# Sums of w2's quarters in the last three experts: ScalarE copies and adding DMAs in place of GpSimd additions

## The chip, the core and the metric

The kernel runs on one core of a Trainium2 chip. A core has TensorE (PE, matrix products), VectorE (DVE), ScalarE (ACT), GpSimd (POOL) and SyncE (SP), which work side by side and wait for each other through semaphores, and 16 DMA engines that move data. DMAs are issued by SP, ACT or POOL. The metric is the device time of one execution in microseconds.

## The reference

The program is an attention block without a softmax followed by a layer of eight experts.

```python
kv = np.einsum('bhsd,bhse->bhde', k, v)
out = np.einsum('bhsd,bhde->bhse', q, kv)
x = out / sqrt(mean(out * out) + 1e-6) * g_norm      # then reshaped to 4608 rows of 512
logits = x @ w_gate                                  # 4608 x 8
# all (row, expert) pairs in falling order of logit: a row takes the expert
# if the row is still free and the expert has fewer than 576 rows
for e in range(8):
    mask = assigned == e
    h = np.maximum(x[mask] @ w1[e], 0.0)             # 576x512 by 512x1024
    out[mask] = h @ w2[e]                            # 576x1024 by 1024x512
```

All tensors are fp32. Every expert receives exactly 576 rows.

## The kernel before, in words

The attention block fills the first 115 us or so. Then the kernel finds which rows belong to which expert, one expert after the other, and from about 148 us on it computes the experts in the order t = 0 to 7. The finding of the later experts' rows is spread over the expert computation in small pieces of VectorE and TensorE work.

For each expert, SP loads w1 and w2 (2 MB each) into `wpool`, whose w2 tile has two buffers, so the load for one expert waits until the expert two before it is done with its w2. GpSimd gathers the expert's rows with indirect DMAs (`xg`, line 971), TensorE transposes them and ScalarE scales them into `xt` (`turn`, line 1068).

Both layers of an expert are computed by a scheme that replaces eight block products by seven (Strassen-Winograd). Its cost is additional sums of blocks:

- `weight_sums(t, i)` (line 1049) makes four sums of w1's quarters for block row i on GpSimd, in `sw`, with two buffers.
- `w2_sums` makes four sums of the quarters b11, b12, b21, b22 of w2 in the tile `tw`: t1 = b12 - b11, t2 = b22 - t1, t3 = b22 - b12, t4 = t2 - b21. Each is 128 partitions by 4 x 256 numbers, and each is made in two halves (line 1199).
- `sums(m)` (line 1113) makes four sums of the hidden values, in `sh`.

The first layer (`one_layer`) runs over four block rows i, with seven products (i, m) each. The order around the end of the first block row is (0,1), (0,2), (0,6), (0,5), (0,7), (0,4), (1,1), (1,2), (0,3), (1,6), and so on. Products 1, 6 and 7 of a block row accumulate in one PSUM bank `x`, which has a single buffer: ScalarE copies the bank to SBUF after each of the three (line 1166), and the next product that goes into that bank waits for the copy. Products 5 and 3 use the banks `z`, and 2 and 4 the banks `y`, with two buffers each. VectorE combines the copies and the banks into `hid`, and ScalarE applies the relu (line 1136). The second layer (line 1121) reads `hid`, `sh`, w2 and `tw`: t1, t2, t3 and t4 are the right operands of its products 5, 6, 7 and 4.

The work on w2 is placed inside the first layer: at each product (i, 1), the code first calls `weight_sums(t, i + 1)`, and then makes the i-th of the four sums t1 to t4. So t1 stands at the start of an expert, t2 at (1,1), t3 at (2,1) and t4 at (3,1).

Three rules set the order. The instructions of TensorE, VectorE and ScalarE run on each engine exactly as written (`manual_schedule`). Those of GpSimd are chained one behind the other by `in_order`, also as written; this chain holds the sums, the gathers and the indirect writes of the results (`put`, line 1088). An engine runs its own list strictly in order, so an instruction that waits holds up everything behind it.

## Time and profile before

| | |
|---|---|
| median of 3 runs | 645.24 us |
| lowest and highest run | 640.3 and 661.66 us |
| profiled execution | 646.56 us |
| its span | 644.8 us |
| busy: PE, DVE, ACT, POOL | 601.7, 379.3, 202.0, 386.0 us |
| mean granted clock of TensorE | 0.964 |
| first layers of experts 5, 6, 7 begin at | 463.3, 521.5, 579.6 us |

The profile is of one execution. Its page gives the busy time of each engine, a picture of the span in 40 slices, the chain of work that ended last, and groups of instructions by source line with their number, busy time and mean duration. The trace behind it can be asked for the instructions in order of time, for the waits, and for the busy time in any stretch. "x32" behind a group is the number of instructions; in square brackets stands the idle time of the engine before an instruction, and what ended it. [...] each product of the code appears as several matrix instructions. "PEld" is the loading of weights into TensorE, which overlaps the matrix instructions. "PEclk" is the clock that was granted to TensorE, 1.00 for full speed.

### The profile page before, as it was taken

How to read it: one execution, taken by the hardware profiler on the slowest of the kernel's cores; microseconds unless marked ns; L12 is line 12 of the kernel's file. 1: busy time of each engine (PE TensorE's matmuls, PEld its weight loads, DVE VectorE, ACT ScalarE, POOL GpSimd, SP SyncE). 2: the span in 40 equal slices, each digit the busy share in tenths (PEclk: the TensorE clock that was granted, in tenths of full speed). 3: DMA queues.
4: the chain of work that ended last, by engine and by line, in shares of the span. 5: the costliest groups of instructions: out<-in, count | busy, mean ns of one | idle time of the engine just before them, and what ended most of it. 6: DMA issues, size and time to landing. Idle time of an engine off the chain costs nothing.

```text
span 644.8 us, 12774 instructions
## 1 busy us (share of the span) xinstructions
PE 601.7 (93%) x4914; PEld 467.5 (73%) x4924; DVE 379.3 (59%) x1242; ACT 202.0 (31%) x432; POOL 386.0 (60%) x402
## 2 busy tenths in 40 slices
PE   7898989348999999999999999999999999999994
PEld 4777878225787678777867786778678777867873
DVE  4366659776886778489568857966671062132101
ACT  1465657922321222223122312231232223122310
POOL 1136434006875597489729873887498579749822
PEclk9899989559999999999999999999999999999998
DMA  8899999438018107210911181027105410910001
GB/s 269 282 320 295 319 291 348 180 127 259 11 50 301 58 2 266 101 43 1 325 43 42 38 297 42 34 72 264 52 23 175 165 69 1 322 53 33 2 10 65
DMA packets 49853, 91.03 MB, mean 141 GB/s; under 512 B 3712, under 2 KB 20096, under 8 KB 49792
## 3 DMA queue, kind: packets, MB, share of 16 engines
q1 hardware_dynamic: 43200, 71.31, 32.4%
q0 software_dynamic: 5888, 18.88, 8.6%
q8 instruction: 39, 0.64, 0.4%
q14 instruction: 22, 0.18, 0.1%
q10 hardware_dynamic: 704, 0.02, 0.1%
HBM read 71.32 MB, written 18.87 MB: 140 GB/s over the span
## 4 chain that ended last, share of the span: by engine, by line
PE 81%; DVE 8%; issue 5%; DMA 2%; POOL 1%; ACT 1%; POOLq 0%; SPq 0%; DVEq 0%; ACTq 0%
PE x_ps L1161 13%; PE x_ps L1121 12%; PE z_ps L1161 9%; PE y_ps L1161 9%; PE y_ps L1121 8%; PE z_ps L1121 7%; PE o_ps L494 4%; PE y_ps L1223 4%; PE qt_ps L382 3%; PE t_ps L1063 3%; PE kv_ps L397 3%; DMA v_sb<-in_v_dram 2%; PE given_ps L675 1%; PE given_ps L670 1%; PE warm_ps L905 1%
## 5 line engine op out<-in xcount | busy, mean ns | idle before, releaser
L1166 ACT COPY h<-x_ps 128x288 f32<-128x288 f32 x93 | 37.2, 400 | 166.0 <-PE x_ps L1161 159.6
L1161 PE MATMUL x_ps<-xs,sw 128*128 128x288 f32 x248 | 71.4, 409 | 0.4 <-DVE xs L1076 0.4
L1088 POOL DMA_INDIRECT out_dram<-y_sb,outs x32 | 31.5, 985 | 56.9 <-DVE y_sb L1259 41.0
L1121 PE MATMUL x_ps<-tw,sh 128*128 128x256 f32 x256 | 61.7, 384 | 0.0
L1161 PEld LDWEIGHTS x_ps<-xs,sw 128*128 128x128 f32 x248 | 46.1, 190 | 13.5 <-issue 1.1
L1068 ACT ACTIVATE xt<-t_ps,g_col 128x512 f32<-128x512 f32 (+3 forms) x41 | 25.8, 635 | 90.8 <-PE t_ps L1063 90.0
L1113 POOL TENSOR_TENSOR sh<-hid 128x512 f32<-128x512 f32 x32 | 40.7, 1271 | 19.8 <-ACT hid L1136 19.8
L1121 PEld LDWEIGHTS x_ps<-tw,sh 128*128 128x128 f32 x256 | 47.0, 190 | 7.4 <-issue 1.4
L1049 POOL TENSOR_TENSOR sw<-w_sb 128x256 f32<-128x256 f32 x64 | 46.8, 731 | 8.1 <-PE z_ps L1161 7.8
L1136 ACT ACTIVATE hid<-hid 128x576 f32<-128x576 f32 x64 | 43.8, 686 | 22.8 <-DVE hid L1175 12.6
L530 POOL TENSOR_TENSOR xo<-o_sb,inv 128x512 f32<-128x512 f32 x27 | 28.4, 1081 | 34.0 <-DVE inv L517 34.0
L971 POOL DMA_INDIRECT xg<-x_dram,ids x40 | 38.2, 955 | 15.6 <-issue 10.2
L1199 POOL TENSOR_TENSOR tw<-w_sb 128x512 f32<-128x512 f32 x32 | 40.1, 1274 | 6.2 <-DMA w_sb<-in_moe_w_dram 6.2
L494 PE MATMUL o_ps<-kvx,qt 64*128 64x72 f32 (+1 forms) x640 | 39.5, 272 | 2.1 <-issue 1.6
L494 PEld LDWEIGHTS o_ps<-kvx,qt 64*128 64x128 f32 (+1 forms) x640 | 34.9, 180 | 7.5 <-issue 5.9
L1161 PE MATMUL z_ps<-xt,sw 128*128 128x288 f32 x128 | 38.0, 414 | 0.0
L1161 PE MATMUL x_ps<-xt,w_sb 128*128 128x288 f32 x124 | 37.3, 415 | 0.5 <-ACT xt L1068 0.5
L1161 PE MATMUL y_ps<-xt,w_sb 128*128 128x288 f32 x128 | 36.8, 408 | 0.0
L1161 PE MATMUL z_ps<-xs,sw 128*128 128x288 f32 x128 | 36.8, 409 | 0.0
L507 DVE TENSOR_REDUCE ms<-sq 128x8 f32<-128x512 f32 x36 | 24.3, 681 | 20.9 <-ACT sq L500 20.5
L1161 PE MATMUL y_ps<-xs,w_sb 128*128 128x288 f32 x128 | 36.5, 407 | 0.0
L1253 ACT COPY u<-x_ps 128x512 f32<-128x512 f32 x24 | 14.0, 584 | 67.3 <-PE x_ps L1121 52.6
(308 smaller groups left out, 1326.4 us busy)
## 6 DMA issues: line engine op xcount, KB each, us to landing
w_sb<-in_moe_w_dram SPq DMA_DIRECT2D x32, 512.0 KB
w_sb<-in_moe_w_dram SPq DMA_DIRECT2D x8, 2048.0 KB
k_sb<-in_k_dram SPq DMA_DIRECT2D x16, 576.0 KB
v_sb<-in_v_dram SPq DMA_DIRECT2D x16, 576.0 KB
q_sb<-in_q_dram SPq DMA_DIRECT2D x16, 576.0 KB
x_dram<-xo SPq DMA_DIRECT2D x16, 512.0 KB
x_dram<-xo SPq DMA_DIRECT2D x4, 256.0 KB
xg<-x_dram,ids POOLq DMA_INDIRECT x40
```

What stands on the lines that cost most here:

```text
L494: nc.tensor.matmul(o_ps[rows_at, rp, (2 * r2 + l) * W:(2 * r2 + l + 1) * W], lhsT=turned_q[bn][ks, l, block // 2:block // 2 + m].rearrange ...
L530: nc.gpsimd.tensor_tensor(xo[:, t], o_sb[:, t, :, 0:D], inv[:, t * H:(t + 1) * H].rearrange("p (h o) -> p h o", o=1).to_broadcast([P, H, D ...
L971: tokens = nc.gpsimd.indirect_dma_start(out=xg[0:nr], out_offset=None, in_=x_dram, in_offset=bass.IndirectOffsetOnAxis(ap=ids[0:nr, n:n + ...
L1049: in_order(nc.gpsimd.tensor_tensor(o, x, y, op=op))
L1068: nc.scalar.mul(xt[:, :, a + c:a + d], t_ps[:, :, c:d], g_col)
L1088: put = nc.gpsimd.indirect_dma_start(out=out, out_offset=bass.IndirectOffsetOnAxis(ap=ids_of[t][0:nr, n:n + 1], axis=0), in_=y_sb[0:nr, :] ...
L1113: in_order(nc.gpsimd.tensor_tensor(o[:, ms], x[:, ms], y[:, ms], op=op))
L1121: nc.tensor.matmul(p_ps[:, n], lhsT=left[:, f, n * P:(n + 1) * P], rhs=right[:, f], start=first, stop=(f == FH - 1), skip_group_check=True)
L1136: nc.scalar.activation(both, both, ACT.Relu)
L1161: nc.tensor.matmul(p_ps, lhsT=lhs[:, r], rhs=rhs[:, r], start=(m in (1, 2, 4, 5) and r == 0), stop=(r == 1), skip_group_check=(m in (6, 7, ...
L1166: nc.scalar.copy(u, p_ps)
L1199: in_order(nc.gpsimd.tensor_tensor(o, x, y, op=AL.subtract))
```

## The change

In experts 5, 6 and 7 the sums t1 to t4 are no longer made by GpSimd additions. For a sum o = x - y, ScalarE first writes -y into o (`nc.scalar.mul(o, y, -1.0)`), and then a DMA that GpSimd issues adds x to what stands in o (`accum_op=AL.add`). In expert 5 a sum is made in one piece (128 x 1024 numbers, 512 KB), in experts 6 and 7 in two halves (256 KB each). The places in the written order stay: the copy goes on ScalarE's list in front of product (i, 1), the DMA on GpSimd's chain behind `weight_sums(t, i + 1)`. Experts 0 to 4 keep the additions.

For t2, y is t1, so ScalarE's copy for t2 reads what the DMA of t1 has written; for t4, x is t2, so the DMA of t4 reads what the DMA of t2 has written. The copies of t1, t3 and t4 read quarters of w2.

In the changed file the added copy is line 1203, the adding DMA line 1204 and the remaining additions line 1200; lines before 1198 keep their numbers, later ones move by five.

```diff
-        w2_sums = [(o[:, m:m + 2], x[:, m:m + 2], y[:, m:m + 2])
-                   for o, x, y in ((t1, b12, b11), (t2, b22, t1), (t3, b22, b12), (t4, t2, b21)) for m in range(0, FH, 2)]
+        whole = ((t1, b12, b11), (t2, b22, t1), (t3, b22, b12), (t4, t2, b21))
+        w2_sums = [(o[:, m:m + 2], x[:, m:m + 2], y[:, m:m + 2]) for o, x, y in whole for m in range(0, FH, 2)]
...
                 if m == 1:
                     if i + 1 < FH:
                         weight_sums(t, i + 1)
-                    for o, x, y in w2_sums[2 * i:2 * i + 2]:
-                        in_order(nc.gpsimd.tensor_tensor(o, x, y, op=AL.subtract))
+                    if t < E - 3:
+                        for o, x, y in w2_sums[2 * i:2 * i + 2]:
+                            in_order(nc.gpsimd.tensor_tensor(o, x, y, op=AL.subtract))
+                    else:
+                        for o, x, y in whole[i:i + 1] if t == E - 3 else w2_sums[2 * i:2 * i + 2]:
+                            nc.scalar.mul(o, y, -1.0)
+                            in_order(nc.gpsimd.dma_start(o, x, accum_op=AL.add))
                 yield from product(i, m)
```

## The prediction

> **What bounds the kernel now.** I read the page's engine sums first, then busy time in one stretch per expert, then the instructions of TensorE, ScalarE and GpSimd in order of time around the point where the edit sits. From the page:

> ```profile
> PE 601.7 (93%) x4914; PEld 467.5 (73%) x4924; DVE 379.3 (59%) x1242; ACT 202.0 (31%) x432; POOL 386.0 (60%) x402
> L1199 POOL TENSOR_TENSOR tw<-w_sb 128x512 f32<-128x512 f32 x32 | 40.1, 1274 | 6.2 <-DMA w_sb<-in_moe_w_dram 6.2
> ```

> TensorE is busy for 93% of the span; GpSimd for 60%. The additions to be replaced cost 1.274 us each. What matters is the last three experts, whose first layers begin at 463.3, 521.5 and 579.6 us. Columns are stretch, length, busy time of PE, PEld, DVE, ACT and POOL with instruction counts, then granted clock, DMA share and GB/s:

> ```profile
> 463.00:521.00 58.00, 58.00 (x269) 45.35 (x268) 21.60 (x59) 15.22 (x29) 43.34 (x45) 1.00 0.33 114
> 521.00:579.00 58.00, 58.00 (x269) 45.33 (x268) 17.33 (x40) 15.12 (x29) 43.36 (x45) 1.00 0.33 113
> ```

> TensorE is busy for all 58.00 us of both stretches at full clock. GpSimd, at 43 of 58, is never what TensorE waits for there (no wait of TensorE on POOL is listed at all). So relieving GpSimd has no wait to remove; a gain would have to come from somewhere else, and every wait that reaches TensorE here is paid in full.

> Now the order around the second copy, in expert 5 (start, length, instruction):

> ```profile
> 468.59 0.40 ACT L1166 COPY h<-x_ps 128x288 f32<-128x288 f32 x1 [1.70 <-PE x_ps L1161]
> 470.75 0.40 ACT L1166 COPY h<-x_ps 128x288 f32<-128x288 f32 x1 [1.75 <-PE x_ps L1161]
> ...
> 467.76 0.73 POOL L1049 TENSOR_TENSOR sw<-w_sb 128x256 f32<-128x256 f32 x1
> ...
> 470.63 2.50 POOL L1199 TENSOR_TENSOR tw<-w_sb 128x512 f32<-128x512 f32 x2
> ...
> 469.44 1.22 PE L1161 MATMUL x_ps<-xt,w_sb 128*128 128x288 f32 x4
> 470.49 1.13 PE L1161 MATMUL y_ps<-xt,w_sb 128*128 128x288 f32 x4
> 471.46 1.13 PE L1161 MATMUL z_ps<-xt,sw 128*128 128x288 f32 x4
> 472.43 1.13 PE L1161 MATMUL x_ps<-xs,sw 128*128 128x288 f32 x4
> ```

> The PE rows are products (1,1), (1,2), (0,3), (1,6) of the first layer. (1,6) accumulates into the bank that (1,1) wrote, so it may start only after ScalarE's copy of (1,1), the one at 470.75. That copy has slack: it may end as late as 472.4. GpSimd reaches the first w2 sum, t1, at 470.63 because the writes of the previous expert and the four sums of weight_sums stand ahead of it.

> [...] For the first expert's second gather of 256 KB, which TensorE waits for:

> ```profile
> 146.01 0.95 POOL L971 DMA_INDIRECT xg<-x_dram,ids  x1 [0.30 <-issue]
> ...
> 149.50 0.42 PEld L1063 LDWEIGHTS t_ps<-ident,xg 128*128 128x128 f32 x4 [0.85 <-DMA xg<-x_dram,ids]
> ```

> That is 3.5 us from issue to first use; I take the trace. [...] No accumulating DMA is in this trace. [...] The last matmul before the routing stage ended at 113.07, and in the stretches after it (columns as above; the last number but two is the granted clock):

> ```profile
> 113.50:114.00 0.50, 0.00 (x0) 0.00 (x0) 0.40 (x1) 0.07 (x1) 0.00 (x0) 1.00 1.02 356
> 114.00:114.50 0.50, 0.00 (x0) 0.00 (x0) 0.14 (x1) 0.50 (x2) 0.00 (x0) 0.67 1.02 385
> 144.50:145.00 0.50, 0.50 (x3) 0.15 (x1) 0.43 (x4) 0.00 (x0) 0.46 (x1) 0.61 0.79 262
> 638.00:640.00 2.00, 0.00 (x0) 0.00 (x0) 0.00 (x0) 0.00 (x0) 0.00 (x0) 0.96 0.29 111
> ```

> The mean of 0.67 puts the fall 0.17 us into its stretch, 1.1 us after the last matmul. At the end matmuls stop at 635.6 and the clock falls at 639.84, 4.2 us later. Dense matmuls began again at 142.02 and the clock came back at 144.89: 2.9 us at half speed, 1.45 us of work lost.

> **The change part by part.**

> *Removed.* 24 additions (8 per expert, three experts) x 1.274 = 30.6 us of GpSimd. Gain on TensorE's path: zero, from the 58.00 of 58.00. What hides them now is TensorE's own work.

> *GpSimd's new work.* 20 DMA issues (4 in expert 5, 8 each in experts 6 and 7). The gather's 0.95 us for 128 rows against 0.91 for 64 rows says the row count hardly matters, so 1.0 to 1.3 each: 20 to 26 us, and each issue behind t1 also waits for its ScalarE copy. GpSimd gets no longer; its first-layer sums L1113 keep their slack (484.78 to 489.8, used by TensorE at 497.8). Cost zero. Without that cover the 2 to 3 us by which the second issue waits would count.

> *ScalarE's copies.* 4 x 1.04 + 16 x 0.61 = 13.9 us, on an engine with 15 of 58 busy. t1's copy comes after the last transposed copy (460.8) and before the copy at 464.55: free. Those of t3 and t4 wait for no DMA (their operands are w2's quarters). In expert 5 t3's copy follows the relu that ends at 476.94, runs to 478.0, and moves the next copy of x from 477.54 to 478.0; it ends at 478.4 and is needed at 479.2. Free, with 0.8 us to spare; in experts 6 and 7 two copies of 0.61 take the same room. t4's, one round later, likewise.

> *The new wait.* t2 = b22 - t1 is now a copy of -t1, so ScalarE waits until the DMA that completes t1 has landed. In ScalarE's hand-written order it stands between the copies at 468.59 and 470.75. Queued behind it: the copy of (1,1), for which (1,6) on TensorE waits, and behind that everything. Deciding time: t1 must be landed by 472.4 - 0.4 - 1.04 = 471.0, but GpSimd issues it only at 470.63. It can't be earlier, as nothing ahead of it on GpSimd changes.

> Expert 5: one DMA of 512 KB. From the gather, 3.5 us for 256 KB. Data itself: the write-backs of 256 KB issued at 465.48 move from about 467.0 at a share of 1.02 and 0.44 of two half microseconds, so 0.73 us each. Fixed part 3.5 - 0.7 = 2.8. 512 KB plain is 1.45. [...] I take 2.9, twice the plain[...]. Landed at 470.63 + 2.8 + 2.9 = 476.3; copy to 477.35; x copy to 477.75. Stall 477.75 - 472.43 = 5.3 us.

> Experts 6 and 7: two DMAs of 256 KB, the second issued 1.3 later (465.48 to 466.77 for two writes). Issue at 528.77: the second lands at 528.77 + 1.3 + 2.8 + 1.45 = 534.3; the second half's copy 0.61 and the x copy 0.40 end at 535.3; (1,6) stood at 530.57. Stall 4.8. Expert 7: issue at 586.89, (1,6) at 588.32, so 592.4 + 1.0 - 588.32 = 5.1. Sum of three stalls 15.2 us.

> *The clock.* TensorE stands still for about 5 us three times; that is beyond both falls seen (1.1 and 4.2 us). Each costs 1.45: 4.4 us. [...]

> *The second load of w2.* Expert 7's w2 reuses the buffer of expert 5, so SP's load now also waits for the DMAs and copies that read it. They are over by about 490; the load goes out at 550. Free.

> Sum: 15.2 + 4.4 = 19.6. Span 644.8 becomes 664.4, the profiled execution 646.56 becomes 666.2; that execution was 1.3 above the median of 645.24, on which it is 664.8. I say **665**.

> **The rivals.**

> *Not slower: the round trip is short.* The single mechanism is t1's landing time. [...] It decides when the sum of stalls and clock is under 12.9 us, so fixed plus moving at 1.6 us below my value. For it: the first gather ran beside the weight load. Against: two gathers both show 3.5, and an earlier fall of the clock after 1.1 us. Chance 0.14.

> *The adding DMA is slow.* At four times the plain moving time the landing is 2.9 us later in each expert (5.8 for 1.45 + 1.45 in the pair): 15.2 + 8.7 + 4.4 = 28.3, 673.5. [...] Against: DMA engines are idle there (share 0.00 from 470 to 480). Chance 0.20.

> *The wait is not there, or GpSimd's relief pays.* ScalarE would have to take t2's copy elsewhere; its written order says not. 645, or 640 with some gain. Chance 0.03.

> **How the numbers follow.** The forecast (657 to 670) has 0.63. The range runs from 654 (the short trip's value; about a tenth is below) to 677 (a quarter-rate DMA plus clock at its upper bound; a tenth above). Slower by over 2%, about what a measurement of this kernel can tell from no change, begins at 658.1: nearly all of the forecast and the slow DMA, 0.84. Within 2%: the short trip, 0.14. Faster: 0.02.

> **What would show it.** ScalarE's wait for a DMA into tw ahead of t2's copy, 7 us from its last instruction in expert 5; TensorE waiting for ScalarE at L1161 three times, 4 to 6 us each, just after (0,3); a granted clock of 0.5 for some 3 us afterwards; no wait before t3's or t4's copies that reaches TensorE; 40 additions left of 64. It is wrong if t1 lands within 2 us of its issue, if the clock stays at 1.00 through the stalls, or if TensorE waits also at the second layer for a late tw.

## The result

| | before | after |
|---|---|---|
| median | 645.46 us (4 runs, 640.3 to 661.66) | 663.84 us (4 runs, 661.77 to 667.47) |
| ratio | | 1.0322, 95% interval 1.0256 to 1.0389 |
| profiled execution | 646.56 us | 663.61 us |
| its span | 644.8 us | 661.8 us |

The changed kernel is slower by 3.2%; the forecast was 665 us. Some executions of one and the same kernel are some per cent longer than the others, as the one of 661.66 us before; the ratios here and below leave these out. The page after, with the line that answers to the one shown of before:

```profile
PE 606.9 (92%) x4914; PEld 470.4 (71%) x4924; DVE 381.2 (58%) x1242; ACT 213.8 (32%) x452; POOL 379.0 (57%) x398
```

ScalarE has 20 instructions and 11.8 us more, GpSimd 4 instructions and 7.0 us less, and TensorE the same 4914 instructions. The waits name the loss (engine, tile and line, then what ended the wait: us in total, times, longest):

```profile
ACT tw L1203 <- DMA tw<-w_sb: 20.7, 5, 7.2
PE x_ps L1161 <- ACT h L1166: 14.9, 3, 5.1
```

Neither stood in the profile of before. ScalarE waits for the DMAs that complete t1 (one in expert 5, two each in experts 6 and 7), and three times TensorE waits for ScalarE's copy behind it. In the order of time, in expert 5 (this execution reached expert 5 about 3 us earlier than that of before):

```profile
465.64 0.40 ACT L1166 COPY h<-x_ps 128x288 f32<-128x288 f32 x1 [1.70 <-PE x_ps L1161]
473.27 1.06 ACT L1203 ACTIVATE tw<-tw 128x1024 f32<-128x1024 f32 x1 [7.23 <-DMA tw<-w_sb]
474.23 0.38 ACT L1166 COPY h<-x_ps 128x288 f32<-128x288 f32 x1
...
467.67 1.40 POOL L1204 DMA_DIRECT2D tw<-w_sb  x1
...
468.51 1.14 PE L1161 MATMUL z_ps<-xt,sw 128*128 128x288 f32 x4
474.76 2.15 PE L1161 MATMUL x_ps<-xs,sw 128*128 128x288 f32 x4 [5.11 <-ACT h L1166]
```

The DMA of t1 goes out at 467.67 and has landed at 473.27, 5.6 us later. The copy of -t1 follows, then the copy of product (1,1), and only then (1,6) starts. Counted from the start of the expert's first layer it starts at 14.38 us (474.76 less 460.38) in place of 9.10 (472.43 less 463.33), so 5.3 us later. The idle time of 5.11 in the line is 0.16 less than that, because the rows of successive products overlap by 0.16 (they begin 0.97 apart and are listed with 1.13). In experts 6 and 7 the delay grows by another 4.9 and 5.3 us: 15.4 in all.

The four matrix instructions of (1,6) take 2.15 us in place of 1.13: the clock has fallen. In stretches of busy time (columns as in the prediction; the last but two is the clock):

```profile
474.50:475.00 0.50, 0.24 (x1) 0.28 (x2) 0.36 (x1) 0.11 (x1) 0.37 (x1) 0.87 0.00 0
478.00:478.50 0.50, 0.50 (x3) 0.30 (x3) 0.00 (x0) 0.00 (x0) 0.00 (x0) 0.72 1.19 172
```

A mean of 0.87 in the first stretch puts the fall at 474.87, 5.2 us after the last matmul ended at 469.65 and 0.1 us after matmuls had begun again. The 0.72 puts the return at 478.28. So the clock was low for 3.4 us of work.

**Where the span's 17 us come from.** The part that the change touches is best measured from the start of expert 5's first layer to the issue of the last write to `out`. That is 463.33 to 636.39 before and 460.38 to 654.17 after, so 173.06 and 193.79: 20.7 us more. The rest is in unchanged code: this execution came to expert 5 2.95 us earlier and ended 0.7 us sooner after its last write. I call these 173.06 us "the last part" and compare all runs by it, since the earlier stages differ by a few us from one execution to the next. Each figure is of one profiled execution. Where nothing differs in this part it comes out alike (173.06 in three of the kernels below, 181.90 and 181.92 in two executions of one); where the clock took another course, two executions of one kernel differ by 1 us.

### The profile page after: what moved, and what is told of

It is laid out like the page before. It is cut to its first block, busy times and chain, and to the rows that moved or that the text cites. A ratio compares the mean times of both kernels' runs of the same rounds, so it can differ in the third digit from the quotient of the medians.

```text
span 661.8 us, 12824 instructions
## 1 busy us (share of the span) xinstructions
PE 606.9 (92%) x4914; PEld 470.4 (71%) x4924; DVE 381.2 (58%) x1242; ACT 213.8 (32%) x452; POOL 379.0 (57%) x398
## 4 chain that ended last, share of the span: by engine, by line
PE 77%; DVE 9%; DMA 4%; POOL 3%; issue 3%; ACT 2%; POOLq 0%; SPq 0%; DVEq 0%; ACTq 0%
PE x_ps L1121 13%; PE x_ps L1161 11%; PE z_ps L1161 9%; PE y_ps L1121 8%; PE y_ps L1161 7%; PE z_ps L1121 6%; PE y_ps L1228 5%; PE o_ps L494 4%; PE qt_ps L382 3%; PE t_ps L1063 3%; DMA tw<-w_sb 2%; PE kv_ps L397 2%; DMA v_sb<-in_v_dram 2%; POOL out_dram L1088 2%; PE given_ps L675 1%
## 5 line engine op out<-in xcount | busy, mean ns | idle before, releaser
L1161 PE MATMUL x_ps<-xs,sw 128*128 128x288 f32 x248 | 74.3, 423 | 15.5 <-ACT h L1166 14.9
L1166 ACT COPY h<-x_ps 128x288 f32<-128x288 f32 x93 | 37.0, 398 | 154.5 <-PE x_ps L1161 148.1
L1161 PEld LDWEIGHTS x_ps<-xs,sw 128*128 128x128 f32 x248 | 47.4, 195 | 30.3 <-issue 17.4
L1049 POOL TENSOR_TENSOR sw<-w_sb 128x256 f32<-128x256 f32 x64 | 48.1, 751 | 28.7 <-PE z_ps L1161 28.4
L1113 POOL TENSOR_TENSOR sh<-hid 128x512 f32<-128x512 f32 x32 | 42.6, 1331 | 23.6 <-ACT hid L1136 23.6
L530 POOL TENSOR_TENSOR xo<-o_sb,inv 128x512 f32<-128x512 f32 x27 | 28.3, 1078 | 35.8 <-DVE inv L517 35.8
L971 POOL DMA_INDIRECT xg<-x_dram,ids x40 | 38.4, 960 | 15.6 <-issue 10.2
L1161 PE MATMUL z_ps<-xs,sw 128*128 128x288 f32 x128 | 39.3, 433 | 0.0
L1161 PE MATMUL z_ps<-xt,sw 128*128 128x288 f32 x128 | 38.0, 414 | 0.0
L1161 PE MATMUL x_ps<-xt,w_sb 128*128 128x288 f32 x124 | 37.3, 415 | 0.5 <-ACT xt L1068 0.5
L1161 PE MATMUL y_ps<-xt,w_sb 128*128 128x288 f32 x128 | 36.8, 408 | 0.0
L1161 PE MATMUL y_ps<-xs,w_sb 128*128 128x288 f32 x128 | 36.5, 408 | 0.0
L1170 DVE TENSOR_TENSOR hid<-z_ps,h 128x288 f32<-128x288 f32 x32 | 14.5, 454 | 37.9 <-ACT h L1166 37.8
```

What stands on the lines that cost most here:

```text
L530: nc.gpsimd.tensor_tensor(xo[:, t], o_sb[:, t, :, 0:D], inv[:, t * H:(t + 1) * H].rearrange("p (h o) -> p h o", o=1).to_broadcast([P, H, D ...
L971: tokens = nc.gpsimd.indirect_dma_start(out=xg[0:nr], out_offset=None, in_=x_dram, in_offset=bass.IndirectOffsetOnAxis(ap=ids[0:nr, n:n + ...
L1049: in_order(nc.gpsimd.tensor_tensor(o, x, y, op=op))
L1113: in_order(nc.gpsimd.tensor_tensor(o[:, ms], x[:, ms], y[:, ms], op=op))
L1161: nc.tensor.matmul(p_ps, lhsT=lhs[:, r], rhs=rhs[:, r], start=(m in (1, 2, 4, 5) and r == 0), stop=(r == 1), skip_group_check=(m in (6, 7, ...
L1166: nc.scalar.copy(u, p_ps)
```

## The experiments

| kernel | last part, us | over before | TensorE's waits ahead of (1,6) in the last three experts, us | ratio to before |
|---|---|---|---|---|
| before | 173.06 | | none | |
| after | 193.79 | 20.73 | 5.11, 4.72, 5.10 | 1.0322 (1.0256 to 1.0389) |
| reorder | 173.06 | 0.00 | none | 0.9950 (0.9881 to 1.0020) |
| late_copy | 173.19 | 0.13 | none | 0.9947 (0.9863 to 1.0030) |
| fill | 188.88 | 15.82 | 0.16 in all | 1.0225 (1.0154 to 1.0296) |
| dma_first | 181.90 | 8.84 | 2.26, 1.90, 2.27 | 1.0109 (1.0020 to 1.0197) |
| dma_first_again | 181.92 | 8.86 | 2.26, 1.89, 2.27 | 1.0117 (1.0077 to 1.0157) |
| only_last | 180.24 | 7.18 | 5.12 | none |
| only_last_again | 181.20 | 8.14 | 5.13 | 1.0106 (1.0076 to 1.0136) |
| no_sums | 173.06 | 0.00 | none | 1.0003 (0.9979 to 1.0026) |
| no_add | 185.16 | 12.10 | 2.87, 2.58, 2.97 | 1.0227 (1.0142 to 1.0313) |

The ratio is to the kernel before on the same chip, with its 95% interval. The expectations for reorder, late_copy, fill and dma_first count the last part to the end of the span: 181.5 us before and 201.4 with the change. The table ends it at the last write's issue, which is 8.4 us less before and 7.7 less in these four and in the changed kernel.

**Same work, without the reading of a fresh sum by ScalarE.** Made from the changed kernel; t3 first, and t2 from t3:

```diff
+        if t >= E - 3:
+            whole = ((t3, b22, b12), (t2, t3, b11), (t1, b12, b11), (t4, t2, b21))
...
-                            nc.scalar.mul(o, y, -1.0)
+                            nc.scalar.mul(o, y, 1.0 if i == 1 else -1.0)
```

> The same copies and adding DMAs, but in the last three experts t3 = b22 - b12 is made first and t2 as b11 + t3, so no ScalarE copy reads what a DMA writes (t2's DMA waits for t3's on GpSimd instead). If the wait of ScalarE's t2 copy is the whole cause: no wait of TensorE on ScalarE at L1161, clock 1.00, from the start of expert 5's first layer to the end of the span 181.5 us as before (201.4 with the change), time 645.5. If the copies or the DMA traffic themselves slow TensorE or the other engines: part of the 20 us stays, 650 or more.

Measured: 173.06 us for the last part, the same as before, and 643.48 us in the median against 648.0 for the kernel before on that chip. All 20 copies and all 20 adding DMAs are still there. ScalarE's copy for t2 and GpSimd's DMA for it:

```profile
468.51 1.06 ACT L1205 ACTIVATE tw<-w_sb 128x1024 f32<-128x1024 f32 x1
470.37 0.40 ACT L1168 COPY h<-x_ps 128x288 f32<-128x288 f32 x1 [0.80 <-PE x_ps L1163]
...
476.41 0.91 POOL L1206 DMA_DIRECT2D tw<-tw  x1 [1.19 <-DMA tw<-w_sb]
```

The wait for the landed sum has moved to GpSimd's list, is 1.19 us long there, and costs nothing. So the copies, the DMA issues and the DMA traffic cost nothing in this order; the cost is one dependency on ScalarE's list.

**The same wait, later in the list.** t2's copy and DMA at product (1,4):

```diff
-                        for o, x, y in whole[i:i + 1] if t == E - 3 else w2_sums[2 * i:2 * i + 2]:
+                        for o, x, y in () if i == 1 else whole[i:i + 1] if t == E - 3 else w2_sums[2 * i:2 * i + 2]:
...
+                if (i, m) == (1, 4) and t >= E - 3:
+                    for o, x, y in whole[1:2] if t == E - 3 else w2_sums[2:4]:
+                        nc.scalar.mul(o, y, -1.0)
+                        in_order(nc.gpsimd.dma_start(o, x, accum_op=AL.add))
```

> t2's copy and DMA moved to product (1,4), about 6 us later in the written order; all else as in the change, the copy still waits for t1's DMA. Wait theory: t1 lands about 0.4 us before or after ScalarE gets there; t2's and t3's copies (2.1 us together) then stand in front of one x copy and cost 0 to 0.5 us per expert; last part 181.5 to 183, time 645.5 to 647. If not the place but the copying costs: near 664.

Measured: 173.19, so 0.13 us in three experts. The dependency remains, and is free where the DMA has landed by the time ScalarE gets to it.

**Work in the pause.** To part the stall from the clock:

```diff
+                if (i, m) == (1, 6) and t >= E - 3:
+                    warm(23)
```

> 23 dummy matmuls (about 5 us) on TensorE in front of product (1,6) in the last three experts, nothing else changed, so TensorE works through the stall. Wait plus clock theory: the three stalls stay lost (14.9 us), the clock stays at 1.00 and its 5.1 us come back: last part 196.5, time 658.7. If the loss is the wait alone and the low clock is harmless: 201.4 and 663.8, or more.

Measured: 188.88 (196.6 to the end of the span, 196.5 expected), 4.9 us less than the changed kernel, with TensorE doing nothing useful in the added matmuls. The medians alone, 661.56 and 663.84 us, are too close to show it. The clock in the place of the stall:

```profile
473.00:474.00 1.00, 0.95 (x5) 0.55 (x5) 0.90 (x4) 0.00 (x0) 0.32 (x2) 1.00 0.41 59
477.00:478.00 1.00, 1.00 (x7) 0.41 (x6) 0.00 (x0) 0.78 (x1) 0.00 (x0) 1.00 0.00 0
480.00:481.00 1.00, 1.00 (x6) 0.78 (x5) 0.74 (x6) 0.98 (x2) 0.00 (x0) 1.00 0.59 86
```

It stays at 1.00. (1,6) starts 5.3, 5.0 and 5.3 us later than before, 15.6 in all against 15.4 in the changed kernel, so the added matmuls fill the stalls and hardly lengthen them. What came back is therefore 4.9 + 0.2 = 5.1 us, and that is what the low clock cost in the changed kernel: 1.7 for each fall, half of the 3.4 us that it lasted. The sum is 15.4 of delay, 5.1 of clock and 0.2 that is lost just behind the three starts of (1,6), in fill too, 20.7 together.

**t1 sooner on its way.** GpSimd issues t1's DMA ahead of `weight_sums(t, 1)`:

```diff
-                    if i + 1 < FH:
+                    if i + 1 < FH and not (t >= E - 3 and i == 0):
                         weight_sums(t, i + 1)
...
                             in_order(nc.gpsimd.dma_start(o, x, accum_op=AL.add))
+                            if i == 0 and (t == E - 3 or o is w2_sums[1][0]):
+                                weight_sums(t, i + 1)
```

> On GpSimd t1's DMA goes out in front of the four sums of weight_sums(t, 1), about 2.9 us earlier; all else as in the change. Wait theory: t1 lands 2.9 us sooner, stalls 2.4, 2.0 and 2.3 (sum 6.7), too short for the clock to fall: last part 188.2, time 652.2. If the clock falls also after 2 us: 193 and 657. If GpSimd's issue time does not set the landing: 201 and 664.

The stalls were 2.26, 1.90 and 2.27 us, each about 2.8 less, where GpSimd issued the DMA 2.9 us sooner (in expert 5, 4.4 us after the start of the first layer in place of 7.3). In the table's measure the expectation is 173.06 + 6.7 = 179.8; that stalls of this length are too short for the clock to fall was an estimate of mine. The last part came out 2 us over it, since the clock fell once, in expert 7:

```profile
473.00:475.00 2.00, 2.00 (x10) 1.55 (x9) 1.29 (x8) 0.98 (x2) 1.18 (x1) 1.00 0.12 17
593.00:595.00 2.00, 2.00 (x7) 1.47 (x7) 0.47 (x2) 0.94 (x2) 2.00 (x4) 0.74 0.00 0
```

After a pause of 2.26 us in expert 5 it is at 1.00 and stays there; after one of 2.27 us in expert 7 it falls at about 594.0, 1.2 us after the matmuls have begun again. The kernel was run once more for this:

> GpSimd's order with t1's DMA first once more, to see three more pauses of TensorE of 2.0 to 2.4 us. If the clock's fall depends on where the pause lies in a window that runs on its own, another number of the three pauses than one may bring it down, and the last part is 173.06 + 6.4 + 1.9 to 2.4 for each fall: 179.5 to 186.7. If the fall belongs to expert 7: again there alone, 181.9.

Again the clock fell in expert 7 alone, and the last part was 181.92. A pause of the same length went without a fall in expert 5 (2.26 us, clock 1.00); the last section sets the pauses beside the times at which the clock changed.

**One expert only.**

```diff
-                    if t < E - 3:
+                    if t < E - 1:
```

> The change in expert 7 alone; experts 5 and 6 keep the GpSimd additions. Wait plus clock theory: one stall of 5.1 us and one fall of the clock at 1.9, 7.0 of the 20.7 us; from the start of expert 5's first layer to the last write's issue 180.1 us (before 173.06, with the change 193.79), time about 652. If the experts hinder each other (queues, buffers) the three don't add up so: 175 or 187.

The profile gave 180.24 for the last part. The four times, 649.5 to 661.85 us, lay too far apart for a ratio, so it was run again more often:

> The change in expert 7 alone once more, since the first runs of it lay between 649.5 and 661.9. If the profile's account is the whole: 7.0 us over the kernel before on the same chip, last part 180.2. If single executions have a further cost that the profiled one missed: 10 us or more over it in the median.

Measured: 1.0106 (1.0076 to 1.0136), or 6.8 us on the 645.7 of before. In its profiled execution the last part was 181.20, 1 us longer than in the first at the same stall (5.13 and 5.12):

```profile
592.00:594.00 2.00, 0.00 (x0) 0.00 (x0) 0.00 (x0) 0.63 (x1) 1.92 (x4) 0.99 1.04 148
594.00:596.00 2.00, 0.54 (x1) 0.50 (x2) 0.66 (x2) 0.92 (x2) 2.00 (x3) 0.50 0.03 5
600.00:602.00 2.00, 2.00 (x8) 1.53 (x7) 0.29 (x1) 0.73 (x2) 0.00 (x0) 0.81 0.00 0
```

Here the clock was low from about 594.0 to 600.8, 6.8 us, twice the 3.4 of the changed kernel and of only_last, and 5.3 of it were work; at half speed that is 2.7 us lost in place of 1.7, which accounts for the 1 us. The stall of expert 7 is the same with and without the change in experts 5 and 6 (5.12 and 5.13 against 5.10), and its part of the changed kernel's 20.7 us is 7.0, so the three experts don't hinder each other.

**What GpSimd's relief is worth.** The kernel before, with the additions of experts 5 to 7 left out and nothing in their place:

```diff
-                    for o, x, y in w2_sums[2 * i:2 * i + 2]:
+                    for o, x, y in w2_sums[2 * i:2 * i + 2] if t < E - 3 else ():
```

> The kernel before without any w2 sums in experts 5, 6 and 7 (their second layer reads the sums of expert 4, so the computation of these sums is left out). My theory that GpSimd's additions are hidden: 173.06 us for the last part, 645 in time, no gain. The rival that relief of GpSimd pays: at least 1 us less, up to the 30.6 us of its additions.

Measured: 173.06 for the last part, and a ratio of 1.0003 (0.9979 to 1.0026). Taking all of these additions away gains nothing, so no replacement for them in these three experts could gain by relieving GpSimd.

**What the adding costs.** Plain DMAs of the same shape; this kernel leaves out the subtraction:

```diff
-                            in_order(nc.gpsimd.dma_start(o, x, accum_op=AL.add))
+                            in_order(nc.gpsimd.dma_start(o, x))
```

> The change with plain DMAs of the same size and shape in place of the adding ones (the subtraction is left out: tw receives x alone). If adding doubles the moving time: 512 KB land after about 4.0 us (5.6 with adding), the second of two of 256 KB after 4.8 (5.65); stalls 3.5, 3.9 and 4.3, sum 11.7, plus 0 to 3 falls of the clock at 1.9: last part 185 to 190.5, time 657 to 662. If adding costs nothing in moving time: stalls 14.9, last part 193.8, time 664.

The stalls were shorter than the theory said, 2.87, 2.58 and 2.97 (the last ended by the four sums on GpSimd, which stand behind two DMA issues). They add up to 8.4 of the 12.1 us. Most of the rest is one fall of the clock, in expert 7, for 6.8 us:

```profile
590.00:591.00 1.00, 0.00 (x0) 0.00 (x0) 0.00 (x0) 0.68 (x2) 1.00 (x3) 0.87 0.01 0
597.00:598.00 1.00, 1.00 (x5) 0.75 (x4) 0.00 (x0) 0.29 (x1) 0.00 (x0) 0.72 0.00 0
```

The means put the fall at 590.74 and the return at 597.56. TensorE's pause ran from 588.61 to 591.57, so here the clock fell within it, 2.1 us after the last matmul. After the pauses of 2.87 and 2.58 us in experts 5 and 6 it stayed at 1.00.

The list of DMA issues, with the median time from issue to landing at the end, first of the changed kernel:

```profile
tw<-w_sb POOLq DMA_DIRECT2D x12, 256.0 KB, 4.1
tw<-w_sb POOLq DMA_DIRECT2D x3, 512.0 KB, 5.5
```

and of the one with plain DMAs:

```profile
tw<-w_sb POOLq DMA_DIRECT2D x12, 256.0 KB, 2.7
tw<-w_sb POOLq DMA_DIRECT2D x3, 512.0 KB, 3.4
```

Adding costs 1.4 us at 256 KB and 2.1 at 512 KB. Part of it is on GpSimd, where an issue takes 1.31 us with and 0.73 us without adding (medians of the 15 from w2); the rest is in the moving, here of t1 in expert 5, in the changed kernel:

```profile
470.00:471.00 1.00, 0.00 (x0) 0.00 (x0) 0.86 (x4) 0.00 (x0) 0.92 (x2) 1.00 1.19 172
471.00:472.00 1.00, 0.00 (x0) 0.00 (x0) 0.91 (x2) 0.00 (x0) 1.00 (x3) 1.00 1.19 172
```

and with plain DMAs:

```profile
466.00:467.00 1.00, 0.78 (x4) 0.27 (x2) 0.90 (x4) 0.00 (x0) 0.12 (x1) 1.00 0.86 299
467.00:468.00 1.00, 0.00 (x0) 0.00 (x0) 0.83 (x5) 0.00 (x0) 0.92 (x2) 1.00 0.66 225
```

The last two numbers are the DMA share and GB/s: 172 GB/s at a share of 1.19 against 299 at 0.86, so about half the rate or a little less.

## Why the prediction was right

*Nothing to gain.* "Gain on TensorE's path: zero, from the 58.00 of 58.00" is shown by no_sums. A row of busy time that is full for the whole stage was enough to say it here.

*The wait.* The place and the order of the wait came out as argued: ScalarE's t2 copy for t1's landing, behind it the copy of (1,1), behind that (1,6). Shown by reorder (the dependency gone, everything else there: 0.00 us) and late_copy (the dependency there, but late: 0.13 us).

*Its size.* Stalls of 5.3, 4.8 and 5.1 were forecast, as the delay of (1,6)'s start; that delay measured 5.3, 4.9 and 5.3. The sum of the landing time was right (5.7 forecast, 5.6 measured for 512 KB), but by luck: two errors cancelled. The fixed part of 2.8 us was taken from a gather that ran while weights were being loaded, and a plain 512 KB DMA would by it have landed after 4.25 us; no_add shows 3.4. The extra for adding was put at 1.45 us, all in moving, an estimate of mine that took the moving for twice as long and that the trace of before, without any adding DMA, did not show; it measured 2.1, of which some 0.6 is GpSimd's issue and 1.5 the moving. A row of another kind of transfer, under another load, was a worse price than it looked.

*The clock.* Forecast 4.4 us, measured 5.1 (fill): 1.7 in place of 1.45 for each fall. The clock was low for 3.4 us of work, not for the 2.9 of the one recovery seen before. This term is the larger part of what parts 20.7 from the forecast's 19.6; the delays are 0.2 more than forecast, and the 0.2 behind the starts of (1,6) had no term. How the fall comes about was not right. The prediction took it for a matter of the time since the last matmul, but the two falls that it showed came 1.1 and 4.2 us after the last matmul, and in the runs a pause of 2.27 us went with a fall (dma_first) while one of 2.87 did not (no_add); the last section has what the traces show.

*The time.* 665 against a median of 663.84 us is closer than the sums behind it. The part that the change touches grew by 20.7 us in place of 19.6, and the rest of the profiled execution happened to be 3.7 us shorter than that of before.

*What was costed at nothing* (the copies of t1, t3 and t4, GpSimd's issues, SP's load) was nothing: reorder has all of it at 173.06. The copies, which I had estimated at 1.04 and 0.61 us, took 1.05 and 0.62 for 1024 and 512 numbers a partition from w2, and 1.06 and 0.63 from `tw`.

*The rivals.* The short round trip, whose 654 us was an estimate that the trace of before did not show, was half true: plain DMAs do land sooner than I took them to (3.4 us for 512 KB in place of 4.25), but adding ones do not (5.6 us, 5.7 forecast); and of three stalls just under 3 us in no_add (2.87, 2.58 and 2.97) two stayed at full clock and one did not. The quarter-rate DMA didn't come: 172 GB/s against 299, about a half. Two of the prediction's figures don't follow from its own sums. The 12.9 us at which the short trip decides is reached 0.8 us below the landing time taken if the clock never falls, and 2.2 below it with three falls, not at 1.6. And a quarter-rate DMA with the 1.7 us per fall that fill shows gives 674.2, not the 677 of the range.

## What to carry to other kernels

When work moves to an engine that is "only 25% busy", look at what that engine's list has next, not at its share: one instruction in an in-order list that waits for a DMA just issued holds up everything behind it until the data have landed (here 5.6 us after the issue; 7.2 us of ScalarE's time and 5.1 of TensorE's). If the dependency must be there, let the instruction that waits be on a list with slack (here GpSimd's), or put it where the data have landed; both cost next to nothing here (0.00 us in reorder, 0.13 in late_copy). And before any relief of a helper engine, ask whether the engine that sets the time ever waits for it; leaving the work out altogether is a quick test.

## What the runs showed of the hardware that I had not expected

| kernel, expert | pause of TensorE | marks | longest idle time between two marks, us | clock |
|---|---|---|---|---|
| dma_first, 5 | 469.97 to 472.23 | 471.08 | 1.15 | stays |
| dma_first, 6 | 530.61 to 532.50 | 532.52 | 1.90 | stays |
| dma_first, 7 | 590.49 to 592.76 | 590.55, 593.96 | 2.21 | falls at 593.96 |
| dma_first_again, 5 | 475.72 to 477.98 | 476.65 | 1.32 | stays |
| dma_first_again, 6 | 536.37 to 538.25 | 538.09 | 1.72 | stays |
| dma_first_again, 7 | 596.26 to 598.53 | 599.53 | 2.27 | falls at 599.53 |
| no_add, 5 | 466.78 to 469.65 | 467.85 | 1.80 | stays |
| no_add, 6 | 528.03 to 530.61 | 529.29 | 1.32 | stays |
| no_add, 7 | 588.61 to 591.57 | 590.73 | 2.12 | falls at 590.73 |

  In these nine, up to 1.90 us of idle time between two marks went without a fall, and 2.12 or more with one at the next mark, while TensorE was still idle in no_add and 1.0 to 1.2 us after it had begun to work again in the two runs of dma_first. In these two the marks lie alike, to 0.2 us, against the pauses of expert 7. The five pauses of 4.7 to 5.1 us of the changed kernel, only_last and only_last_again left 3.2 to 3.4 us of idle time between two marks, and each went with a fall.

  The clock came back after one step, 3.41 us, in the changed kernel, where TensorE had begun again 0.1 to 0.2 us ahead of each fall, and after two, 6.8 us, in only_last_again and in no_add, where 1.5 and 0.8 us of the first step were still idle. All this is read from the traces afterwards, among the experts' products alone, and no run was made to test it. Earlier in the program, in the kernel before, the clock fell at 114.17 after 1.1 us without matmuls, and came back at 144.89 with 0.7 us of the step ahead of it idle.
